# Start of a fused DeltaNet and SwiGLU kernel: weight loads two at a time, idle-time products on TensorE, separate PSUM banks for chunk 0, q loaded behind the first squares

## The chip, the cores and the metric

The kernel runs on one core of a Trainium2 chip. The metric is the device time of one execution, in microseconds (us); the number compared is the median over several executions. One further execution was recorded by the hardware profiler, and all durations below come from it. The engines are PE (TensorE, with PEld for its weight loads), DVE (VectorE), ACT (ScalarE), POOL (GpSimd) and SP (SyncE, which here only issues transfers). Each engine works through its own list of instructions in order.

## The reference

Two blocks follow each other. The first is a delta rule over 768 time steps, for 4 batches times 8 heads of size 48. The second is a feed-forward block on the 3072 rows that come out, 384 wide inside the model and 1536 wide in the hidden layer.

```python
k_n = k / (norm(k, axis=-1) + 1e-06)
state = zeros((B, H, D, D))                      # B=4, H=8, S=768, D=48
for t in range(S):
    y[:, :, t] = einsum('bhd,bhde->bhe', q[:, :, t], state)
    v_old = einsum('bhde,bhd->bhe', state, k_n[:, :, t])
    state = state + beta[:, :, t] * einsum('bhd,bhe->bhde', k_n[:, :, t], v[:, :, t] - v_old)

x = y.transpose(0, 2, 1, 3).reshape(3072, 384)
g = x @ w_gate                                   # 384 x 1536
out = (g * sigmoid(g) * (x @ w_val)) @ w_out     # 1536 x 384
```

q, k, v and beta are 32-bit numbers; the three weight matrices arrive as 64-bit numbers.

## The kernel before

Time is cut into 12 chunks of 64 steps. Inside a chunk the recurrence becomes a triangular system: the Gram matrix of the keys is built, its triangular part is inverted (the result is called Z), and then products give the corrected values `u`, the output `y` and the new state. The feed-forward block of a chunk runs on the same core, in between the attention products of later chunks. From about 85 us on PE is never idle for long; the start, which the change edits, is different, because chunk 0 has to get through a chain of dependent steps before there is any feed-forward work to do.

All instructions are put in an order written out by hand, engine by engine (`tc.manual_schedule`). So the order in which the Python calls stand is the order on every engine, and an instruction that waits holds back all that stand behind it on its engine. The start runs as follows.

1. Loads. `k` of chunks 0 and 1 is issued from the SP and ACT queues before anything else (chunk 0 in four transfers, line 188; chunk 1 by `load_k`, line 135). `beta` goes from POOL (line 395). Then, all on SP: `q` of chunk 0 into `qpad[0]`, `k` of chunks 2 and 3, `q` of chunk 1, `v` of chunk 0 (line 181), the first 12 pieces of weights (`stage`, line 258), `v` of chunk 1, and two more pieces.
2. Norms of the keys (`norms`, lines 368 to 380): DVE squares and sums, POOL takes a power (line 380). Between the two calls stands a memset of the padding columns of `qpad[0]` (line 1580).
3. PE transposes `k` of chunk 0 (line 470), ACT copies the result (line 472), PE forms the Gram products (lines 623 and 624), and the same for chunk 1. ACT and DVE pick out the diagonal blocks (line 629), and DVE transposes them (line 1603).
4. `first_scale` joins the norms with the Gram blocks (lines 422 to 649), and `first_substitution` (lines 665 and 671) runs 15 steps of two DVE operations each; `first_z` and `spread_z` (lines 675 to 686) write Z. Meanwhile PE transposes `q` and the later keys and forms their Gram products (line 486). The last of these is that of `q` of chunk 1.
5. `advance(0)`: PE multiplies Z into the lower blocks (line 695) and into `v` (line 904), then refines the result three times, half by half (`by_par`, line 924, with a DVE addition, line 1288, after every half), and forms `y` of chunk 0 with the products of `by_par` again (also line 924). `y` has two halves called `par`. Half 0 is copied by ACT (line 999); half 1 is copied in four parts by ACT and DVE in turn (line 1002), all from one PSUM bank. Then PE transposes `y` into `x` (line 1017), and ACT copies it in two parts (line 1020). After that the first feed-forward product (`gate_val`, line 1217) can start.

The weights arrive as 64-bit words in staging places and are turned into 32-bit numbers by two ACT operations (`power_step`, lines 270 and 276) and three DVE operations (`convert`, lines 287 to 307) a piece. `converts_first` does this for the first six pieces by hand, among the steps of `advance(0)`.

PSUM is used as two double banks with the tags `px` and `py`, and four single banks `ffn0` to `ffn3`, which `ps_ffn` hands out in turn or by number.

Of the kernel before, what the change touches and what calls it, by code (L numbers as in the profile page):

```python
# [20 lines left out]
def kernel(  # L21
# [47 lines left out]
    def ps_pair(name, tag):  # L69

        return psum.tile([128, 2, 512], FP32, name=name, tag=tag, bufs=1)
# [58 lines left out]
    def halves(x, c, b):  # L130
        return x[NB * b : NB * b + NB, :, c * C : (c + 1) * C, :]
# [43 lines left out]
    def load_v(c):  # L175
        vin[c] = work.tile([128, 2, NB, NJ, D], FP32, name="vin", bufs=2)
        for b in range(2):
            src = halves(v, c, b).rearrange("bp (j par) p d -> par p (bp j) d", par=2)
            for par in range(2):
                s = 64 * (b ^ par)  # L180
                nc.sync.dma_start(
                    out=vin[c][s : s + 64, par].rearrange("p bp j d -> p (bp j) d"),
                    in_=src[par],
                )

    for bp in range(NB):
        for b, engine in enumerate((nc.sync, nc.scalar)):
            engine.dma_start(
                out=knp[0][64 * b : 64 * b + 64, bp, :, 0:D],
                in_=halves(k, 0, b)[bp].rearrange("h p d -> p h d"),  # L190
            )
    load_k(1, (nc.sync, nc.scalar))
    beta_b = const.tile([128, NG, R], FP32, name="beta_b")
    wg_sb = const.tile([128, KT, DFF], FP32, name="wg_sb")
# [48 lines left out]
        at = max(before) if before else LATE.get(name, -1)  # L243
        freed_by.setdefault(at, []).append(n)

    def stage(n, queue=nc.sync):
        _, src, t, f0, m = pieces[n]
        name, lo = place_of[n]
        if name not in places:
            if name == "p_sb":  # L250
                places[name] = words(p_places[0])
            else:
                places[name] = work.tile(
                    [128, 2 * PIECE], U32, name="staged", tag=name, bufs=1
                )
        place = places[name][:, lo : lo + 2 * m]
        staged[n] = place
        queue.dma_start(
            out=place, in_=src[t * 128 : (t + 1) * 128, f0 : f0 + m].bitcast(U32)
        )  # L260
# [88 lines left out]
    def half_of(x):  # L349
        return slice(64 * x, 64 * x + 64)  # L350
# [13 lines left out]
    def norms(c):  # L364

        ksq = work.tile([128, NB, H, D], FP32, name="ksq", tag="r", bufs=2)
        x = knp[c][:, :, :, 0:D]
        nc.vector.tensor_tensor(out=ksq, in0=x, in1=x, op=ALU.mult)
        n = n_t[0][:, c].rearrange("p (par bp j) -> p par bp j", par=2, bp=NB)
        ksq_v = ksq.rearrange("p bp (j par) d -> p par bp j d", par=2)  # L370
        for to, of, par in (
            (slice(0, 128), slice(0, 128), 0),
            (half_of(0), half_of(1), 1),
            (half_of(1), half_of(0), 1),
        ):
            nc.vector.tensor_reduce(
                out=n[to, par], in_=ksq_v[of, par], axis=mybir.AxisListType.X, op=ALU.add
            )
        n = n_t[0][:, c]
        nc.gpsimd.tensor_tensor(out=n, in0=n, in1=half[:, 0:HH], op=ALU.pow)  # L380
# [225 lines left out]
    def unread():  # L606

        p = ps_pair("p_t", "px")[:, 0]
        for n in range(88):
            q_ = QUADS[n % 4][0]  # L610
            nc.tensor.matmul(p[q_, 0:1], half[q_], half[q_, 0:1])

    def first_gram(c, tag):

# [239 lines left out]
    def advance(c):  # L854
# [7 lines left out]
        if c > 0:  # L862
# [23 lines left out]
        p_u = recur(ps_pair("p_u", "px"))  # L886

        def new_u(name):
            return work.tile([128, 2, NB, NJ, D], FP32, name=name, tag="r", bufs=2)

        def single(bank):
            return [
                p[:, 0 : NB * NJ * D].rearrange("p (bp j d) -> p bp j d", bp=NB, j=NJ)
                for p in banks("p_u", bank)
            ]

        v0 = new_u("uu" if c > 1 else "v0")
        if c == 0:
            p_n = banks("p_n", "py")
# [2 lines left out]
                n_copy(c, p_n, par)  # L902
        for bp, j, par, b, first in every():
            nc.tensor.matmul(  # L904
                p_u[half_of(b), par, bp, j],
                zt[half_of(b ^ par), par, bp, j],
                r[half_of(b ^ par), par, bp, j],
                start=first,
                stop=True,
                skip_group_check=True,  # L910
            )
# [7 lines left out]
        def by_par(p, stationary, moving, flip, start):  # L919
            for par in range(2):  # L920
                for bp in range(NB):
                    for j in range(NJ):
                        for b in range(2):
                            nc.tensor.matmul(  # L924
                                p[par][half_of(b ^ par * flip), bp, j],
                                stationary[half_of(b), par, bp, j],
                                moving[half_of(b), par, bp, j],
                                start=start and bp + j == 0,
                                stop=True,
                                skip_group_check=True,  # L930
                            )
                yield par

        if c < 2:
            yield MORE
            uu = new_u("uu")
            p_n = single(2) if c == 0 else [p_u[:, par] for par in range(2)]
# [53 lines left out]

        if 0 < c < NCH - 1:
            of_state()
        each = range(NB) if c == 0 else (slice(0, NB),)
        y = work.tile([128, NB, NJ, 2, D], FP32, name="y", tag="r", bufs=2)
        if c == 0:
            for par in by_par(p_y, pq, uu, 1, True):
                if par == 0:
                    nc.scalar.copy(y[:, :, :, 0], p_y[0])
            for bp in range(NB):  # L1000
                for b, copy in ((0, nc.scalar.copy), (1, nc.vector.tensor_copy)):
                    copy(y[half_of(b), bp, :, 1], p_y[1][half_of(1 - b), bp])
        else:
            p_of_u()
            nc.scalar.copy(y[:, :, :, 0], p_y[:, 0])
            for b in range(2):
                nc.scalar.copy(y[half_of(b), :, :, 1], p_y[half_of(1 - b), 1])
# [4 lines left out]
        p_f = ps_pair("p_f", "py")[:, :, 0 : KT * 128]  # L1012
        p_f = p_f.rearrange("p bp (t n) -> p t bp n", t=KT)
        for bp in range(NB):
            for t in range(KT):
                at = slice(t * 128, (t + 1) * 128)
                nc.tensor.transpose(p_f[:, t, bp], y_f[:, bp, at], ident)  # L1017
        x_v = xts[c].rearrange("p t (bp n) -> p t bp n", bp=NB)
        for bp in each:
            nc.scalar.copy(x_v[:, :, bp], p_f[:, :, bp])  # L1020
        if 2 <= c < NCH - 1 and (c + 1) // 2 in n_t:
            scale_v(c + 1)
        yield
# [543 lines left out]
    with tc.manual_schedule(  # L1567
# [9 lines left out]
        load_beta()  # L1577
        first_tiles()
        norms(0)
        nc.vector.memset(qpad[0][:, :, :, D:DP], 0.0)  # L1580
        norms(1)
        load_q(0)
        load_k(2)
        load_k(3)
        load_q(1)
        load_v(0)
        for n in range(12):
            stage(n)
        load_v(1)
        stage(12)  # L1590
        stage(13)
        copy_a, copy_v = nc.scalar.copy, nc.vector.tensor_copy
        unread()
        turned(0, False, 0)
# [7 lines left out]
        spread_beta(copy_a)  # L1602
        nc.vector.transpose(first_of["mb"][:, 0 : R * R], first_of["flat"])
        first_scale(first_n())
        low_copies(0, p_g[0])
        turned(0, True, 0)
        low_copies(1, p_g[1])
# [19 lines left out]
        scale_v(0)  # L1627
        for steps_of in first_q:
            next(steps_of)
        new_nt(0, qpad[1].rearrange("p bp h d -> p (bp h d)"))  # L1630
        zb_1 = work.tile([128, R, R], FP32, name="zb", bufs=1)
        new_nt(1, zb_1.rearrange("p k i -> p (k i)"))
# [94 lines left out]
```

## Time and profile before

| what | value |
|---|---|
| median of 3 executions | 705.18 us (705.01 to 708.58) |
| profiled execution, its own time | 704.64 us |
| its span, first to last instruction | 702.4 us |
| mean granted TensorE clock | 0.993 |
| PE busy | 681.3 us (97% of the span) |
| DVE busy | 472.4 us (67%) |
| ACT busy | 258.8 us (37%) |
| POOL busy | 51.0 us (7%) |
| DMA | 62.32 MB, mean 89 GB/s |

PE is busy in 97% of the span, so what time it loses is found in stretches. The stretches in which PE works less lie in the first 60 us. A start time in the views below is counted from the first instruction; where a row says "issue", the engine stood without waiting for anything that the profile shows.

### The profile page before, as it was taken

What the parts mean: (1) busy time and instruction counts of PE and PEld (TensorE: products, weight loads), DVE (VectorE), ACT (ScalarE), POOL (GpSimd) and SP (SyncE); (2) the same over time, 40 slices, a digit from 0 to 9 for tenths busy, and PEclk for the clock granted to TensorE, in tenths of its full rate; (3) what the DMA queues carried; (4) which work ended last, traced back from release to release, by engine and by line L of the source; (5) the groups of instructions that cost most, each with busy time, mean ns of one, the idle gap of its engine ahead of it and who ended that gap; (6) DMA issues with size and microseconds to landing.
All of it is one profiled execution on the core that took longest, in us unless ns stands there. A gap on an engine that the chain in (4) does not pass through costs nothing.

```text
span 702.4 us, 25672 instructions
## 1 busy us (share of the span) xinstructions
PE 681.3 (97%) x11432; PEld 641.7 (91%) x11432; DVE 472.4 (67%) x1096; ACT 258.8 (37%) x542; POOL 51.0 (7%) x39
## 2 busy tenths in 40 slices
PE   7599999999999999999999999999999999999997
PEld 6588788756999999999999999999999999999997
DVE  5866779798899848987469787379844345333341
ACT  4456666203533433235233235232153132142230
POOL 6000031105000030000300001200000000000000
PEclk9899999999999999999999999999999999999999
DMA  8873715006461522465333274143241131221210
GB/s 140 246 197 85 217 50 185 1 22 149 136 128 24 108 67 59 77 128 93 71 90 70 58 136 81 35 114 83 55 107 48 44 85 57 54 62 46 68 46 23
DMA packets 143886, 62.32 MB, mean 89 GB/s; under 512 B 123008, under 2 KB 126080, under 8 KB 143776
## 3 DMA queue, kind: packets, MB, share of 16 engines
q1 hardware_dynamic: 141552, 60.19, 36.7%
q8 instruction: 90, 1.47, 0.9%
q10 hardware_dynamic: 2096, 0.39, 0.3%
q0 software_dynamic: 128, 0.10, 0.1%
q14 instruction: 20, 0.16, 0.1%
HBM read 53.58 MB, written 7.08 MB: 86 GB/s over the span
## 4 chain that ended last, share of the span: by engine, by line
PE 91%; DVE 3%; ACT 3%; issue 1%; POOL 1%; DMA 1%; SPq 0%; DVEq 0%; ACTq 0%; POOLq 0%
PE ffn L1121 43%; PE ffn L1327 20%; PE ffn L1217 8%; PE ffn L1244 4%; PE p_g L486 3%; PE p_u L904 2%; PE p_s L972 2%; PE p_r L866 2%; PE p_y L960 1%; PE p_y L875 1%; PE ffn L924 1%; PE p_f L1017 1%; POOL n_t L380 1%; PE p_u L924 1%; DMA kn<-in_k_dram 1%
## 5 line engine op out<-in xcount | busy, mean ns | idle before, releaser
L1121 PE MATMUL ffn<-x_ffn,wg_sb 128*128 128x128 f32 x840 | 128.3, 275 | 0.3 <-ACT x_ffn L1020 0.2
L1121 PE MATMUL ffn<-x_ffn,wv_sb 128*128 128x128 f32 x840 | 128.1, 275 | 0.0
L1121 PEld LDWEIGHTS ffn<-x_ffn,wg_sb 128*128 128x128 f32 x840 | 111.1, 192 | 0.6 <-ACT ffn L1177 0.3
L1121 PEld LDWEIGHTS ffn<-x_ffn,wv_sb 128*128 128x128 f32 x840 | 110.7, 192 | 0.0
L1151 ACT ACTIVATE sil<-ffn 128x256 f32<-128x256 f32 x120 | 46.1, 384 | 132.6 <-PE ffn L1121 127.8
L1327 PE MATMUL ffn<-wo_sb,h_f 128*128 128x192 f32 x480 | 83.4, 327 | 0.0
L1156 DVE TENSOR_TENSOR h_f<-sil,ffn 128x256 f32<-128x256 f32 x120 | 49.6, 418 | 48.8 <-ACT sil L1151 46.3
L1327 PEld LDWEIGHTS ffn<-wo_sb,h_f 128*128 128x128 f32 x480 | 78.1, 190 | 0.4
L1288 DVE TENSOR_TENSOR ffn<-ffn,p_sb 128x512 f32<-128x512 f32 x58 | 40.4, 696 | 44.6 <-ACT ffn L1177 43.6
L1121 PE MATMUL ffn<-x_t,h_f 128*128 128x128 f32 x480 | 61.0, 280 | 0.2 <-ACT ffn L1134 0.2
L1121 PEld LDWEIGHTS ffn<-x_t,h_f 128*128 128x128 f32 x480 | 56.2, 191 | 1.4 <-ACT ffn L1134 0.3
L564 DVE TENSOR_TENSOR zb<-zb,tmp 128x31 f32<-128x31 f32 (+15 forms) x155 | 53.1, 343 | 5.3
L558 DVE TENSOR_TENSOR tmp<-zb,mb 128x31 f32<-128x31 f32 (+15 forms) x155 | 52.7, 340 | 4.0
L774 POOL TENSOR_TENSOR n_b<-mb,half 128x32 f32<-128x32 f32 x5 | 30.0, 6002 | 338.5 <-DVE mb L528 338.5
L1288 DVE TENSOR_TENSOR o_sb<-o_sb,ffn 128x192 f32<-128x192 f32 x49 | 17.2, 351 | 51.2 <-PE ffn L1327 49.1
L1134 ACT COPY ffn<-ffn 128x512 f32<-128x512 f32 x30 | 17.1, 571 | 63.8 <-PE ffn L1121 57.4
L1327 PE MATMUL ffn<-last_k,h_f 128*128 128x192 f32 x200 | 35.9, 327 | 0.0
L1217 PE MATMUL ffn<-x_ffn,wg_sb 128*128 128x256 f32 x144 | 34.0, 383 | 0.0
L1217 PE MATMUL ffn<-x_ffn,wv_sb 128*128 128x256 f32 x144 | 33.8, 382 | 0.0
L1327 PEld LDWEIGHTS ffn<-last_k,h_f 128*128 128x128 f32 x200 | 32.9, 190 | 0.1
L1121 PE MATMUL ffn<-x_ffn,p_sb 128*128 128x128 f32 x216 | 30.1, 282 | 1.2 <-issue 1.2
L1217 PEld LDWEIGHTS ffn<-x_ffn,wv_sb 128*128 128x128 f32 x144 | 27.0, 190 | 3.7
(272 smaller groups left out, 1063.6 us busy)
## 6 DMA issues: line engine op xcount, KB each, us to landing
h_f<-w_s SPq DMA_DIRECT2D x60, 256.0 KB, 2.8
p_sb<-w_s SPq DMA_DIRECT2D x27, 256.0 KB, 2.7
vin<-in_v_dram SPq DMA_DIRECT2D x48, 96.0 KB, 3.4
out_dram<-o_sb SPq DMA_DIRECT2D x48, 96.0 KB, 2.2
kn<-in_k_dram SPq DMA_DIRECT2D x19, 192.0 KB, 4.4
zt<-in_moe_w_out_dram SPq DMA_DIRECT2D x6, 384.0 KB, 3.3
qpad<-in_q_dram SPq DMA_DIRECT2D x36, 64.0 KB, 3.0
w_s<-h_f SPq DMA_DIRECT2D x7, 256.0 KB, 3.5
```

Of the source, the lines that this page charges most:

```text
L486: nc.tensor.matmul(p_v[par][half_of(b if of_q else b ^ par), bp, j], kt[c][half_of(par), bp, j, b], xt[half_of(par), bp, j, b],)
L558: nc.vector.tensor_tensor(out=t_v, in0=zb[:, 0 : j + 1, j : j + 1].to_broadcast([128, j + 1, m]), in1=mb[:, j : j + 1, j + 1 : R].to_broad ...
L564: nc.vector.tensor_tensor(out=zb[:, 0 : j + 1, j + 1 : R], in0=zb[:, 0 : j + 1, j + 1 : R], in1=t_v, op=ALU.add,)
L774: nc.gpsimd.tensor_tensor(out=n, in0=mb.rearrange("p j i -> p (j i)")[:, 0 : R * R : R + 1], in1=half, op=ALU.pow,)
L1121: nc.tensor.matmul(p[:, u], w(u), moving, start=start and u == 0, stop=True, skip_group_check=True,)
L1134: nc.scalar.copy(p_y, p_x)
L1151: nc.scalar.activation(sil[:, n].rearrange("p (i n) -> p i n", i=2), p[:, 0:2], ACTF.Silu)
L1156: nc.vector.tensor_tensor(out=h_of(c, f, j), in0=sil[:, n].rearrange("p (i n) -> p i n", i=2), in1=p[:, 2:4], op=ALU.mult,)
L1217: nc.tensor.matmul(ps[name][:, i], w_sb[:, t, (f + i) * 128 : (f + i + 1) * 128], xts[c][:, t], start=(t == 0 and i == 0), stop=(t == KT - 1),
L1244: nc.tensor.matmul(p_o, hs[c, f - f % 2][:, f % 2, bp * 128 : (bp + 1) * 128], wo_sb[:, f], start=(f == 0), stop=(f == FT - 1),)
L1288: nc.vector.tensor_tensor(out=out, in0=a, in1=b, op=ALU.add)
L1327: nc.tensor.matmul(p[x, part], a(f - f % 2)[:, f % 2], b(f), start=not begun and f == 0, stop=f == FH - 1, skip_group_check=True,)
```

## The change

It has five parts.

- `k` of chunk 0 is loaded by two transfers of 192 KB in place of four of 96 KB.
- The memset of `qpad[0]` moves from between the two `norms` calls to between the squares and the sums of `norms(0)`, and it is one column wider. That column is also written by the load of `q` of chunk 0, so this load, on SP, now waits for the memset, and SP's later transfers stand behind it.
- `stage` gets an argument `after`. With it POOL copies one column from the staging place of piece `after` to that of piece `n`, before the transfer of `n`: the copy waits until piece `after` has landed, and the transfer waits for the copy. Pieces 2 to 13 get it, with `n - 2`. These calls stand behind `first_scale` now, so POOL's copies come behind its work for the norms.
- `warm(3)` puts three products of 128x128 by 128x512, whose result nobody reads, on PE between the Gram products of `q` and `advance(0)`. They go into the double bank `px`.
- In chunk 0 the part of `y` with `par` 1 and `bp` 1 goes into a third single bank (`ffn2`). ACT copies the two parts of `bp` 0 and DVE the two of `bp` 1. `x` is transposed into `ffn0` and `ffn3` in place of the double bank `py`; ACT copies one and DVE the other.

```diff
-    for bp in range(NB):
-        for b, engine in enumerate((nc.sync, nc.scalar)):
-            engine.dma_start(
-                out=knp[0][64 * b : 64 * b + 64, bp, :, 0:D],
-                in_=halves(k, 0, b)[bp].rearrange("h p d -> p h d"),
-            )
+    load_k(0, (nc.sync, nc.scalar))
...
-    def stage(n, queue=nc.sync):
+    def stage(n, after=None, queue=nc.sync):
...
+        if after is not None:
+            nc.gpsimd.tensor_copy(place[:, 0:1], staged[after][:, 0:1])
...
         n = n_t[0][:, c].rearrange("p (par bp j) -> p par bp j", par=2, bp=NB)
+        if c == 0:
+            nc.vector.memset(qpad[0][:, :, :, D - 1 : DP], 0.0)
...
+    def warm(count):
+
+        p = ps_pair("p_t", "px")[:, 0]
+        for _ in range(count):
+            nc.tensor.matmul(p, ident, kts[0][:, 0:512])
...
-            for par in by_par(p_y, pq, uu, 1, True):
+            third = single(2)[0]
+            for par in range(2):
+                for bp in range(NB):
+                    p = third if par and bp else p_y[par]
+                    for j in range(NJ):
+                        for b in range(2):
+                            nc.tensor.matmul(
+                                p[half_of(b ^ par), bp, j],
+                                pq[half_of(b), par, bp, j],
+                                uu[half_of(b), par, bp, j],
+                                start=j == 0 and (bp == 0 or par == 1),
+                                stop=True,
+                                skip_group_check=True,
+                            )
                 if par == 0:
                     nc.scalar.copy(y[:, :, :, 0], p_y[0])
-            for bp in range(NB):
-                for b, copy in ((0, nc.scalar.copy), (1, nc.vector.tensor_copy)):
-                    copy(y[half_of(b), bp, :, 1], p_y[1][half_of(1 - b), bp])
+            for b in range(2):
+                nc.scalar.copy(y[half_of(b), 0, :, 1], p_y[1][half_of(1 - b), 0])
+                nc.vector.tensor_copy(y[half_of(b), 1, :, 1], third[half_of(1 - b), 1])
...
+        if c == 0:
+            p_f = [ps_ffn([128, KT, 128], "p_f", 3 * bp) for bp in range(NB)]
+        else:
+            p_f = ps_pair("p_f", "py")[:, :, 0 : KT * 128]
+            p_f = p_f.rearrange("p bp (t n) -> p t bp n", t=KT)
...
+        if c == 0:
+            nc.scalar.copy(x_v[:, :, 0], p_f[0])
+            nc.vector.tensor_copy(x_v[:, :, 1], p_f[1])
+        else:
+            nc.scalar.copy(x_v, p_f)
...
         norms(0)
-        nc.vector.memset(qpad[0][:, :, :, D:DP], 0.0)
         norms(1)
...
-        for n in range(12):
-            stage(n)
-        load_v(1)
-        stage(12)
-        stage(13)
...
         first_scale(first_n())
+        for n in range(12):
+            stage(n, n - 2 if n > 1 else None)
+        load_v(1)
+        stage(12, 10)
+        stage(13, 11)
...
         for steps_of in first_q:
             next(steps_of)
+        warm(3)
```

More of the change, by code (lines that the diff above doesn't have):

```diff
@@ L885, in advance @@
             yield
-        p_u = recur(ps_pair("p_u", "px"))
         def new_u(name):
@@ L895, in single @@
             ]
+        p_u = recur(ps_pair("p_u", "px"))
+        p_u_of = [p_u[:, 0], p_u[:, 1]]
         v0 = new_u("uu" if c > 1 else "v0")
@@ L904, in advance @@
             nc.tensor.matmul(
-                p_u[half_of(b), par, bp, j],
+                p_u_of[par][half_of(b), bp, j],
                 zt[half_of(b ^ par), par, bp, j],
@@ L936, in advance @@
             uu = new_u("uu")
-            p_n = single(2) if c == 0 else [p_u[:, par] for par in range(2)]
+            p_n = single(2) if c == 0 else p_u_of
             for n in range(3):
@@ L993, in advance @@
             of_state()
-        each = range(NB) if c == 0 else (slice(0, NB),)
         y = work.tile([128, NB, NJ, 2, D], FP32, name="y", tag="r", bufs=2)
         if c == 0:
-            for par in by_par(p_y, pq, uu, 1, True):
+            third = single(2)[0]
[12 more added lines that the diff above has]
+                            )
                 if par == 0:
                     nc.scalar.copy(y[:, :, :, 0], p_y[0])
-            for bp in range(NB):
-                for b, copy in ((0, nc.scalar.copy), (1, nc.vector.tensor_copy)):
-                    copy(y[half_of(b), bp, :, 1], p_y[1][half_of(1 - b), bp])
+            for b in range(2):
+                nc.scalar.copy(y[half_of(b), 0, :, 1], p_y[1][half_of(1 - b), 0])
+                nc.vector.tensor_copy(y[half_of(b), 1, :, 1], third[half_of(1 - b), 1])
         else:
@@ L1011, in advance @@
         xts[c] = ffn_pool.tile([128, KT, TOK], FP32, name="x_ffn")
-        p_f = ps_pair("p_f", "py")[:, :, 0 : KT * 128]
-        p_f = p_f.rearrange("p bp (t n) -> p t bp n", t=KT)
+        if c == 0:
[3 more added lines that the diff above has]
+            p_f = p_f.rearrange("p bp (t n) -> p t bp n", t=KT)
         for bp in range(NB):
@@ L1016, in advance @@
                 at = slice(t * 128, (t + 1) * 128)
-                nc.tensor.transpose(p_f[:, t, bp], y_f[:, bp, at], ident)
+                p = p_f[bp][:, t] if c == 0 else p_f[:, t, bp]
+                nc.tensor.transpose(p, y_f[:, bp, at], ident)
         x_v = xts[c].rearrange("p t (bp n) -> p t bp n", bp=NB)
-        for bp in each:
-            nc.scalar.copy(x_v[:, :, bp], p_f[:, :, bp])
+        if c == 0:
[3 more added lines that the diff above has]
+            nc.scalar.copy(x_v, p_f)
         if 2 <= c < NCH - 1 and (c + 1) // 2 in n_t:
```

## The prediction

> **What bounds the kernel now.** First the page: PE is busy 97% of the span, and only the first slices of row PE are below 9. I therefore read only the start. Next the chain that ended last, from 0 to 110 us (start, length, what):
>
> ```profile
> 1.64 6.00 DMA kn<-in_k_dram
> ...
> 10.58 6.73 POOL n_t L380 x2
> ...
> 28.36 1.25 DVE mb L675
> 29.64 0.78 ACT zt L684
> ...
> 33.64 1.53 issue
> 35.17 0.61 PE p_u L904 x25
> ...
> 36.34 8.44 PE ffn L924 x231
> 44.77 0.69 issue
> ```
>
> The keys land at 7.64, the norms end on POOL at 17.30, the substitution gives Z at 29.64, then PE's products follow. PE alone, in order of time, shows what it waited for (in brackets):
>
> ```profile
> 27.00 0.92 PE L486 MATMUL ffn<-qt,kt 64*64 64x64 f32 x24 [2.58 <-issue]
> ...
> 35.17 0.57 PE L904 MATMUL p_u<-vin,zt 64*64 64x48 f32 x25 [1.53 <-issue]
> 36.34 3.28 PE L924 MATMUL ffn<-v,qpad 64*64 64x48 f32 x64 [0.60 <-ACT v L913]
> 39.41 4.28 PE L924 MATMUL ffn<-uu,qpad 64*64 64x48 f32 x128
> ```
>
> "Issue" is a wait for nothing that the profile shows. The stalls stand 128 matmul records (256 instructions) apart or a multiple, and the instruction queue q8 moves one packet in the us around 24, 32 and 43, just before they end. I read them as instruction fetches queued behind weights. The third view is the work by stretches of one us; the last three columns are granted clock, DMA share, GB/s:
>
> ```profile
> 24.00:25.00 1.00, 0.42 (x31) 0.32 (x21) 0.89 (x4) 1.00 (x3) 0.00 (x0) 1.00 0.76 219
> 26.00:27.00 1.00, 0.00 (x0) 0.00 (x0) 0.90 (x4) 0.00 (x0) 0.00 (x0) 0.79 1.03 352
> 28.00:29.00 1.00, 0.00 (x0) 0.00 (x0) 0.93 (x3) 0.00 (x0) 0.00 (x0) 0.50 1.01 379
> 38.00:39.00 1.00, 1.00 (x26) 1.00 (x22) 0.51 (x1) 1.00 (x2) 0.00 (x0) 0.50 1.09 241
> ```
>
> PE runs at half clock from 26.6 to 33.4 and from 36.8 to 40.2 (the ends worked out from means such as 0.79), while DMA is full. So the start loses to late keys, to fetches, and to the clock.
>
> **Part 1: keys of chunk 0, q behind the squares.** The first squares start at 7.75, when the later SP half of k lands (issued 1.64, 6.0 us). Two transfers instead of four end k's issue at about 1.5 instead of 2.5, and q, on SP from 3.29, no longer shares the engines. Ahead of the squares there are then only k of two chunks and beta, 0.88 MB, which at the 165 to 195 GB/s of 3 to 7 us are through by about 7. Chunk 0 has the head start: I estimate 6.0 (5.2 to 7.0). From there two paths lead to the join at line 422 (before, 17.33). Norms: 9.6 us as before plus the memset, 0.3 (row 1580, 0.27), so 9.9. Gram: it had 0.42 us to spare, 9.2; but now all eight transposes follow the landing where four were done before, and four took 1.08: 10.25. This one ends last: 16.25, a gain of 1.1. On SP, q, k of 2 and 3, q of 1 and v of 0 follow the memset, from about 7.3. The 2.9 MB from the first k to that v took from 2 to 22 us, some 145 GB/s, and that pace, not SP, spaced them; so v's end and the first weight (19.8) stay; PE's last Gram product may come a us later, which the wait for Z hides. POOL's 12 copies run beside the substitution. The nearest row is the 128x32 copy on POOL, 0.24 us; if each of the six before Z stopped DVE for so long it would be 1.4, if none, 0. I take 0.3. **Z: 0.8 earlier** (2.0 earlier to 0.5 later).
>
> **Part 2: weights two at a time, and fetches.** The first weights, with few in flight, landed in 3.9 and 3.7 us; with eight, in 6.5:
>
> ```profile
> h_f<-in_moe_w_gate_dram SPq DMA_DIRECT2D x1, 256.0 KB, 3.9
> h_f<-in_moe_w_gate_dram SPq DMA_DIRECT2D x1, 256.0 KB, 6.5
> ```
>
> With two in flight I take 3.2 (quiet 256 KB loads later: 2.8) plus 0.4 for POOL's copy and the SP issue: 3.6 a pair. Pieces 0 and 1 start at 19.8, so 2 and 3 land at 27, 4 and 5 at 30.6, 10 and 11 at 41.4, v of 1 at about 45, 12 and 13 at 46. ACT takes pieces 0 and 2 at 33, pieces 6 on at about 48 and 12 at about 52 (before: 52.9 and 56.87): covered, by 6 us for piece 12. [...] A packet keeps one engine for about 1.3 us (8.3% of 16 engines for one us), then about 1 us passes; only the queueing before it, 1 to 2 us, is what fewer weights save. While PE runs at full clock it also has less time before the next block. So of the 1.53 I leave 1.1, of the 0.69 I leave 0.1.
>
> **Part 3: the unread products.** Full-rate rows of 128x256 give 1.49 us for three (6 records, line 1217), so three of 128x512 take 3.0. PE's Gram work ends near 25.7 with a fetch stall cut to about 1 us, so they fill 25.7 to 28.7, just ahead of the first product with Z (29.7). [...] The row decides: from 23.2 to 26.6 PE worked only 1 us and the clock fell; from 33.4 to 36.8 it worked 1.3 of 3.4 (38%), and it fell again. With the products that first stretch is 70% busy. At full clock 64 products with Z take 1.16 (row 486) instead of 2.2, and p_u 1.15. From Z to the end of p_u: 0.84 + 1.16 + 1.1 stall + 1.1 = 4.2 instead of 6.14: **1.9 earlier** (0.8 to 3.0). The refinements (36.34 to 44.29, 7.95) at the 0.93 a half of the later rows take 6 x 0.93 + 1.2 = 6.75: **1.2 earlier** (0 if the clock falls once more: the stall and the copy of v leave PE about half busy there, between 38% and what surely holds).
>
> **Part 4: y and x.** Last refinement to first feed-forward product: 44.29 to 49.50, 5.2. The four y copies took turns (46.46 to 47.89); now ACT and DVE take two each, 0.7. But DVE's two stand behind the conversion of pieces 0 and 2 (1.75), and its x copy behind that of piece 4 (1.2). Along DVE: 1.75 + 0.7 + 1.2 + 0.55, then PE: 4.25. **0.95 earlier**, of which 0.6 is the fetch (0.3 to 1.6).
>
> **Part 5: what comes later.** Pieces 12 to 22, v of 1 and 2, and q of 2, some 3.9 MB, move from before 48 to about 42 to 54. There PE is dense, and its next blocks end near 45.3 and 48.7. [...] **0.7 later** (0 to 2). After that PE is bound by its work (10.0 busy in each 10 us from 90), and the shift stays to the end.
>
> Sum: -0.8 - 1.9 - 1.2 - 0.95 + 0.7 = -4.15. The profiled 704.64 (span 702.4) becomes 700.5; it stood 0.54 below the median 705.18, which becomes **701.0**.
>
> **Rivals.**
> A (the sum above, 699 to 702.5): 0.62.
> B, the clock still falls, or fetches take as long: the 1.2 and half of the 1.9 are lost: -4.15 + 2.15 = -2.0, 703.2. For it: p_u's stall and the copy of v. Against it: the stretch before Z is filled. 0.15.
> C, the moved burst costs what the throttle saved: two stalls of 1.5 between 45 and 55: 704.0. For it: DMA was empty there before. [...] 0.13.
> D, slower: the throttle makes weights late. ACT needs piece 12; it lands at 19.8 + 7P, P the time of a pair. At P = 5.3 that is 56.9, where it was needed before, and nothing is gained; from 5.8 the run is over 3.5 slower, at 6 it is 5 slower, 710. For it: 6.5 us with eight in flight. Against it: 3.9 with few. 0.10.
>
> **Numbers.** 0.5%, 3.5 us, is about what a measurement can tell (the runs spread by that). A gives 0.50 faster and 0.12 same; B 0.02 and 0.13; C 0.13 same; D 0.10 slower. Faster 0.52, same 0.38, slower 0.10. The range 697.5 to 705.6 takes in the ends of A, then B and C, and leaves out D and A's best ends.
>
> **What would show it.** Squares at about 6; Z near 28.8; granted clock 1.0 from 23 to 45; no 2.58 wait in line 486; first product of line 1217 near 44.7; a new "issue" wait near 49. Wrong, if the products start after 28, if ACT waits for a DMA at pieces 8 to 13, or if the first product of line 1217 comes earlier and the end does not.

## The result: 0.4% faster, and the profile after

| | runs | median us | lowest to highest | profiled execution (span) |
|---|---|---|---|---|
| before | 20 | 706.63 | 705.01 to 709.44 | 704.64 (702.4) |
| changed | 20 | 703.46 | 701.89 to 707.33 | 707.33 (705.6) |

The ratio of changed to before is 0.9958, with a 95% interval of 0.9944 to 0.9971: 2.0 to 4.0 us faster, about 3.0. The forecast was 4.15 faster. The change is real, but at 0.42% it stays below the 0.5% that the prediction asked of "faster", to which it gave 0.52, and counts as its "same", to which it gave 0.38.

The profiled execution of the changed kernel happens to be the longest of its 20, so its waits are read here and its total is not. One of the kernels below, u_yx, has the same program on PE up to the end of the refinements and gives a second look at that stretch.

PE of the changed kernel in order of time (start, length, what; in brackets the idle time before it and what ended it), at the places that the prediction had named:

```profile
5.85 1.94 PE L469 MATMUL ffn<-ident,kn 128*128 128x128 f32 x8 [2.00 <-DMA kn<-in_k_dram]
...
13.60 0.21 PE L629 MATMUL p_g<-kt 64*32 64x64 f32 x1 [1.46 <-issue]
...
27.02 0.57 PE L485 MATMUL ffn<-qt,kt 64*64 64x64 f32 x23 [2.02 <-issue]
27.52 2.84 PE L616 MATMUL p_t<-kt,ident 128*128 128x512 f32 x6
30.39 1.35 PE L700 MATMUL p_n<-zt,a_sb 64*64 64x64 f32 x61
...
34.50 0.68 PE L910 MATMUL p_u<-vin,zt 64*64 64x48 f32 x31 [2.25 <-issue]
35.77 3.65 PE L930 MATMUL ffn<-v,qpad 64*64 64x48 f32 x64 [0.59 <-ACT v L919]
...
49.52 1.53 PE L1242 MATMUL ffn<-x_ffn,wg_sb 128*128 128x256 f32 x6 [0.18 <-DVE x_ffn L1043]
...
56.68 1.01 PE L880 MATMUL p_y<-state,qt 64*64 64x48 f32 x51 [1.76 <-issue]
```

The keys are there at 5.8, as forecast. Everything after that differs from the forecast. The fetch stall ahead of line 485 (486 before) is 2.02 where about 1 was expected, so the unread products (line 616) run from 27.52 to 30.36, up to the very moment when ACT has written its part of Z (30.34). The stall in p_u is 2.25 and not 1.1. The first gate product starts at 49.52, where it stood before (49.50).

The same execution by stretches of one us (busy PE, PEld, DVE, ACT, POOL; granted clock; DMA share; GB/s):

```profile
26.00:27.00 1.00, 0.00 (x0) 0.00 (x0) 0.89 (x4) 0.00 (x0) 0.00 (x0) 1.00 0.45 129
28.00:29.00 1.00, 1.00 (x4) 0.47 (x3) 0.93 (x2) 0.00 (x0) 0.18 (x1) 1.00 0.33 53
33.00:34.00 1.00, 0.00 (x0) 0.00 (x0) 0.85 (x2) 0.00 (x0) 0.00 (x0) 1.00 0.49 180
38.00:39.00 1.00, 1.00 (x24) 1.00 (x22) 0.32 (x1) 1.00 (x2) 0.15 (x1) 0.50 0.35 131
55.00:56.00 1.00, 0.00 (x0) 0.00 (x0) 1.00 (x5) 1.00 (x4) 0.00 (x0) 1.00 0.97 336
```

DMA is no longer full while PE waits for code (0.45 at 26, where it was 1.03), and still PE waits. The clock is whole at 28, where it was half. But PE then idles through the whole of the us from 33, and the clock is half from 35.6 to 42.4: the half clock has moved from before Z to the refinements behind it. In the us from 55, PE idles once more for nothing that the profile shows, while DMA is full; before, no such stall stood here. These "issue" stalls are called waits for code from here on, because a packet of the instruction queue q8 starts 2.3 to 2.9 us before each of them ends. In the trace of the changed kernel 125 to 128 matmul records lie between one of them and the next, or a multiple of that; a block is one such stretch of PE's program, and its end is called a boundary.

### The profile page after: what moved, and what is told of

The parts are those of the page before. It is cut to its first block, busy times and chain, and to the rows that moved or that the text cites. A ratio compares the mean times of both kernels' runs of the same rounds, so it can differ in the third digit from the quotient of the medians.

```text
span 705.6 us, 25724 instructions
## 1 busy us (share of the span) xinstructions
PE 684.5 (97%) x11438; PEld 642.9 (91%) x11438; DVE 473.0 (67%) x1097; ACT 258.7 (37%) x541; POOL 54.0 (8%) x51
## 3 DMA queue, kind: packets, MB, share of 16 engines
q8 instruction: 90, 1.47, 0.9%
## 4 chain that ended last, share of the span: by engine, by line
PE 94%; issue 2%; DVE 2%; ACT 1%; DMA 1%; DVEq 0%; ACTq 0%
PE ffn L1146 42%; PE ffn L1352 20%; PE ffn L1242 9%; PE ffn L1269 4%; PE p_g L485 3%; PE p_u L910 2%; PE p_s L978 2%; PE p_r L871 2%; PE p_y L880 2%; PE ffn L930 1%; PE p_y L966 1%; PE p_u L930 1%; PE p_f L1039 1%; PE ffn L469 1%; PE p_j L848 1%
## 5 line engine op out<-in xcount | busy, mean ns | idle before, releaser
L1146 PEld LDWEIGHTS ffn<-x_ffn,wg_sb 128*128 128x128 f32 x840 | 111.1, 192 | 0.7 <-ACT ffn L1202 0.4
L1146 PEld LDWEIGHTS ffn<-x_ffn,wv_sb 128*128 128x128 f32 x840 | 110.7, 192 | 0.0
L1242 PEld LDWEIGHTS ffn<-x_ffn,wg_sb 128*128 128x128 f32 x144 | 26.6, 190 | 4.3 <-DVE wg_sb L304 0.4
```

The lines of the kernel that those rows point to most:

```text
L1146: nc.tensor.matmul(p[:, u], w(u), moving, start=start and u == 0, stop=True, skip_group_check=True,)
L1242: nc.tensor.matmul(ps[name][:, i], w_sb[:, t, (f + i) * 128 : (f + i + 1) * 128], xts[c][:, t], start=(t == 0 and i == 0), stop=(t == KT - 1),
```

## The experiments

All ratios are to the kernel before on the same chip. A difference between two kernels is the difference of their ratios, with the two intervals combined as independent, turned into us at 706 us a run. "Gate" is the start of the first product of line 1242 in the profiled execution (49.52 in the changed kernel).

### Undoing one part of the changed kernel

**u_warm** leaves out the three unread products.

```diff
         for steps_of in first_q:
             next(steps_of)
-        warm(3)
```

> The changed kernel without the three unread products; all else as changed. The changed kernel stands 3.0 us below the one before (ratio 0.9958). Theory 'the products hold the clock': the granted clock falls to 0.5 before the first product with Z, and the gain shrinks by about 2 us, to -1.0. Rival 'the clock is lost anyway, later, in the stall of p_u and the copy of v' (the changed kernel's own profile had 0.5 from 35.8 to 42.2): without the products the loss only moves, and the gain stays within 0.7 us of -3.0.

Measured: median 701.92 in 11 runs, ratio 0.9946 [0.9925, 0.9967]. Without the products the kernel is 0.8 us faster than with them, plus or minus 1.8: no gain from them can be seen, and the 2 us of the theory are ruled out. The rival comes nearer: the loss only moves. Its PE, in order of time:

```profile
26.39 0.57 PE L485 MATMUL ffn<-qt,kt 64*64 64x64 f32 x23 [0.65 <-issue]
...
30.13 2.12 PE L700 MATMUL p_n<-zt,a_sb 64*64 64x64 f32 x61 [3.16 <-ACT zt L689]
32.13 1.94 PE L910 MATMUL p_u<-vin,zt 64*64 64x48 f32 x62
34.68 2.07 PE L930 MATMUL ffn<-v,qpad 64*64 64x48 f32 x64 [0.61 <-ACT v L919]
```

The mechanism shows. PE idles 3.16 us until Z, the clock falls (half from 30.2 to 33.6), p_n takes 2.12 instead of 1.35, and p_u 1.94. But p_u now has no stall at all (62 products in 1.94 without a wait): while PE crawls, the next code arrives. PE begins the refinements at 34.68, earlier than the 35.77 of the changed kernel, with the clock whole (64 products in 2.07 instead of 3.65), and the gate is at 45.43. With the faster products in front of it, PE waited 2.25 us for that code; without them, not at all.

**u_thr** takes the throttle away: the first 14 loads are issued at once, in their old place, and POOL's copies are gone.

```diff
         load_v(0)
+        for n in range(12):
+            stage(n)
+        load_v(1)
+        stage(12)
+        stage(13)
...
         first_scale(first_n())
-        for n in range(12):
-            stage(n, n - 2 if n > 1 else None)
-        load_v(1)
-        stage(12, 10)
-        stage(13, 11)
         low_copies(0, p_g[0])
```

> The changed kernel with the first 14 pieces of weights loaded without the waits, where the kernel before has them. Theory 'two in flight shortens the fetches before Z and in p_u': the wait of line 485 is back at 2.5 us and that of p_u at 1.5 or more; but the new wait near 55 us (1.8 us in the changed kernel's profile) goes away, so the net loss is small: -2.5 of the -3.0 stays. Rival 'the throttle is where the gain is': -0.5 or less stays, because the unread products then start after 27.5 us and run into the first product with Z.

Measured: 706.47 in 12 runs, 1.0003 [0.9987, 1.002]. The throttle is worth 3.2 us (plus or minus 1.5), about as much as the whole change. That 2.5 us of the gain would stay, as the first theory had it, is wrong, and the rival is right about the time. PE:

```profile
27.52 0.57 PE L485 MATMUL ffn<-qt,kt 64*64 64x64 f32 x23 [2.56 <-issue]
28.02 2.84 PE L616 MATMUL p_t<-kt,ident 128*128 128x512 f32 x6
30.80 1.16 PE L700 MATMUL p_n<-zt,a_sb 64*64 64x64 f32 x64
...
35.03 0.68 PE L910 MATMUL p_u<-vin,zt 64*64 64x48 f32 x31 [2.58 <-issue]
```

With eight loads in flight, the stalls are 0.5 and 0.3 us longer (2.56 for 2.02, 2.58 for 2.25), the first product with Z has to wait for the unread ones until 30.80 although ACT's part of Z is ready at 30.13, and p_u resumes at 35.03. The gate is at 50.01. The throttle's price is visible too: u_thr has no stall near 56, so the stall there in the changed kernel belongs to the moved burst. Up to the gate the trace accounts for some 0.5 us, against 3.2 in the times; set against u_yx, the second look at the changed kernel's start, the refinements end 2.5 us later in u_thr (45.66 for 43.19). How the 3.2 divide is not shown, since single executions differ by as much.

**u_q** puts back the four transfers of k of chunk 0 and the early q.

```diff
-    load_k(0, (nc.sync, nc.scalar))
+    for bp in range(NB):
+        for b, engine in enumerate((nc.sync, nc.scalar)):
+            engine.dma_start(
...
-        if c == 0:
-            nc.vector.memset(qpad[0][:, :, :, D - 1 : DP], 0.0)
...
         norms(0)
+        nc.vector.memset(qpad[0][:, :, :, D:DP], 0.0)
         norms(1)
```

> The changed kernel with k of chunk 0 in four transfers and q straight behind k, as before. Theory 'the earlier keys are eaten by a fetch in the Gram products of chunk 1' (in the changed kernel's profile the squares start 1.9 us earlier, but a wait of 1.5 us in line 628 leaves the join at 17.2 against 17.3): nothing is lost, -3.0 stays within 0.5. Rival, the prediction's step: Z comes 0.8 to 1.1 us later, -2.0 stays.

Measured: 705.31 in 12 runs, 0.999 [0.9971, 1.0009]: this part is worth 2.3 us (plus or minus 1.6), where the theory had nothing and the rival about 1. Its trace shows the squares at 7.78, two us later than in the changed kernel, but Z at 29.68, against 29.54 there and 29.27 to 29.33 in u_warm, u_thr and u_yx, whose start is the same: later by 0.1 to 0.4. Of the two us of earlier keys, little reaches Z, and yet undoing them costs time. What carries the 2.3 us was not located.

**u_yx** puts back the old banks and copies of y and x.

```diff
-            third = single(2)[0]
...
-            for b in range(2):
-                nc.scalar.copy(y[half_of(b), 0, :, 1], p_y[1][half_of(1 - b), 0])
-                nc.vector.tensor_copy(y[half_of(b), 1, :, 1], third[half_of(1 - b), 1])
+            for bp in range(NB):
+                for b, copy in ((0, nc.scalar.copy), (1, nc.vector.tensor_copy)):
+                    copy(y[half_of(b), bp, :, 1], p_y[1][half_of(1 - b), bp])
...
-        if c == 0:
-            nc.scalar.copy(x_v[:, :, 0], p_f[0])
-            nc.vector.tensor_copy(x_v[:, :, 1], p_f[1])
```

> The changed kernel with the y and x copies of chunk 0 as before (one bank for y's second half, a double bank for x). Theory, the prediction's step: from the end of the last refinement to the first product of line 1217/1242 takes 5.0 us instead of 4.25 and the end comes 0.6 to 0.95 later: -2.2 stays. Rival 'ACT's conversions, which run without a break from the copy of the state, set the pace after 52 us and hide it': -3.0 stays.

Measured: 704.67 in 12 runs, 0.9981 [0.996, 1.0001]; 1.6 us lost, plus or minus 1.7, so not separated from nothing. The trace is sharper: from the end of the last refinement (43.19) to the gate (47.65) it takes 4.46, where the theory had 5.0, and in the changed kernel 4.35 (45.17 to 49.52). The banks themselves are worth about 0.1 us.

As the second look at the changed kernel's start, u_yx shows the same picture a little milder: a stall of 1.64 in line 485, of 1.99 in p_u, and half clock from 36.5 to 39.9, so that the refinements take 7.96 us (35.23 to 43.19).

```profile
33.96 0.68 PE L910 MATMUL p_u<-vin,zt 64*64 64x48 f32 x31 [1.99 <-issue]
35.23 2.64 PE L930 MATMUL ffn<-v,qpad 64*64 64x48 f32 x64 [0.59 <-ACT v L919]
```

The four differences add up to 6.3 us, more than the 3.0 of the whole: the parts overlap, and the changed kernel's own error stands in all four.

### Shifting where PE's code blocks end

If PE's wait for code falls where it does because of the count of instructions ahead of it, a few instructions more or fewer should move it. The 88 tiny products at the very start (32x32 by 1, before the keys land) are the place: one fewer is two matmul records, four instructions of PE (b85 below, the kernel before with three fewer, has 11,426 matmul records and as many weight loads, for 11,432).

```diff
-        for n in range(88):
+        for n in range(94):
             q_ = QUADS[n % 4][0]
```

**w94** is the changed kernel with 94; **n94** is the same without warm(3); **b94** is the kernel before with 94; **w82** is the changed kernel with 82.

> The changed kernel with 94 instead of 88 tiny products at the very start (1.0 to 4.0 us, before any key has landed): every later boundary of 256 instructions on PE comes 12 matmul records earlier in the program. So 35 instead of 29 records of a block are done when PE stands at the first product with Z. Theory 'the fetch in p_u is asked for about 32 records into a block, and so only once Z is there': now it is asked for before Z, the wait of 2.0 to 2.6 us in p_u goes away, PE no longer idles, the clock stays at 1.0 through the refinements, and the end comes 2 to 4 us earlier than the changed kernel's: ratio 0.990 to 0.993. Rival 'DMA is simply slow there, whenever the fetch is asked for': the wait moves by 12 records but stays about 2 us, ratio 0.995 to 0.997.

> As w94, without the three unread products. [...] Theory 'the products are worth the half clock once the fetch no longer stands behind them': n94 is 1 to 2 us slower than w94. [...]

> The kernel before with 94 instead of 88 tiny products at the start, nothing else. 36 instead of 24 records of the block lie ahead of the first product with Z. Theory of the early request: the wait of 1.5 us in p_u goes away although all weights are in flight, the clock does not fall a second time, ratio about 0.996 (1.5 for the wait and 1.2 for the clock). Rival 'the weights in flight make the fetch slow': the wait stays at 1 us or more, ratio 0.999 to 1.001.

> The changed kernel with 82 tiny products: boundaries 12 records later, 17 records of the block ahead of Z. Control for w94: theory of the request 32 records in: the wait in p_u, now 46 records into p_u, is 1.6 to 2.2 us still, as the request comes 0.2 us later and the boundary 0.4 us later. If a shift as such helped, it would be gone here too.

| | median us (runs) | ratio | stall in 485 | stall in p_u | gate |
|---|---|---|---|---|---|
| w94 | 703.57 (12) | 0.9965 [0.9942, 0.9988] | 1.87 | 0.49 | 46.42 |
| n94 | 707.07 (12) | 1.0001 [0.9983, 1.0019] | 1.49 | 0.79 | 49.34 |
| b94 | 709.12 (12) | 1.0023 [1.0, 1.0046] | 3.51 | 1.16 | 49.91 |
| w82 | 699.54 (2) | 0.9895 [0.9848, 0.9943] | 1.56 | 1.82 | 47.53 |

PE of w94:

```profile
17.83 1.86 PE L469 MATMUL ffn<-ident,qpad 128*128 128x128 f32 x8 [2.34 <-ACT a_sb L639]
...
28.74 0.80 PE L485 MATMUL ffn<-qt,kt 64*64 64x64 f32 x35 [1.87 <-issue]
29.47 2.84 PE L616 MATMUL p_t<-kt,ident 128*128 128x512 f32 x6
32.24 1.16 PE L700 MATMUL p_n<-zt,a_sb 64*64 64x64 f32 x64
...
34.22 0.90 PE L910 MATMUL p_u<-vin,zt 64*64 64x48 f32 x43 [0.49 <-issue]
35.69 2.07 PE L930 MATMUL ffn<-v,qpad 64*64 64x48 f32 x64 [0.57 <-ACT v L919]
```

The stall in p_u is down to 0.49, and the clock stays whole through the refinements (64 products in 2.07). But it was not the early request that did this. The packet that ends the stall starts at 31.75, no earlier than in the changed kernel (31.65); PE only reaches the end of its block later, at 33.7 instead of 32.25. The time did not follow either; 0.990 to 0.993 had been expected. The shift put a boundary ahead of the transposes of q: they start at 17.83 instead of 16.05, and the 2.34 before them is put down to ACT, but a packet starts at 14.85, and n94 shows a wait at the same place as "issue" (1.46). The clock then fell to half from 17.9 to 21.3. So the unread products start at 29.47 only, and the first product with Z comes at 32.24, 2 us after Z. One good boundary was paid for with a bad one.

n94 shows it from the other side: it is u_warm with six tiny products more, and it is 3.9 us slower (plus or minus 2.0). It is also 2.5 us slower than w94 (plus or minus 2.1), as the theory for n94 had it: here the unread products do seem to help, though the boundaries behind Z differ between the two as well. In b94 the stall in p_u stays, at 1.16, against the theory, and it is 1.6 us slower than the kernel before, at the edge of its interval. w82 shows the 1.6 to 2.2 that were expected of its stall (1.82). So six tiny products more or fewer, which do no work for the result, are worth about as much as the change.

w82 has two runs only. **w82b** is the same kernel with more runs, **b85** the kernel before with 85, and **w85** and **n85** are the changed kernel with 85, with and without the unread products. Three tiny products are six matmul records, and so are the three unread ones. So n85 (three tiny ones fewer and no unread ones) puts the boundaries behind Z where w82b (six tiny ones fewer) has them, and w85 puts them where u_warm has them.

```diff
-        for n in range(88):
+        for n in range(82):
             q_ = QUADS[n % 4][0]
```

> The kernel of w82 (the changed kernel, 82 tiny products at the start) once more, timed in full. Theory 'the place of PE's boundaries of 256 instructions decides': w82's trace shows 0.2 us of 'issue' waits on PE after 62 us, where the changed kernel shows 3.2 and the kernel before 2.1, so it stays 2 to 3 us ahead of the changed kernel: ratio 0.990 to 0.993. Rival 'two runs by chance': ratio 0.9958 as the changed kernel.

> The changed kernel without the three unread products and with 85 tiny products: boundaries after Z as in w82b. Theory 'the products only cost their shift': the same time as w82b within 1 us, ratio 0.990 to 0.993. Theory 'the products hold the clock': 1 to 2 us slower than w82b.

> The changed kernel, all five parts, with 85 tiny products: the three products' 12 instructions are taken out again ahead of them, so that all later boundaries stand where they stand in the kernel before and in u_warm. Theory 'the products cost their shift': the 'issue' waits after 62 us are 2.1 instead of 3.2, and it is 1 us faster than the changed kernel, ratio 0.9945, equal to u_warm. Theory 'the products hold the clock and are worth it': faster than u_warm by 1 or more, ratio 0.993 or less.

> The kernel before with 85 tiny products instead of 88, nothing else: after the place of the three unread products its boundaries stand where they stand in w82. Theory of the boundaries: the 'issue' waits after 62 us fall from 2.1 to about 0.2, ratio 0.997. Rival: the boundaries are worth something only with the other parts: ratio 0.999 to 1.001.

| | median us (runs) | ratio | stall in p_u | waits for code on PE after 62 us | gate |
|---|---|---|---|---|---|
| w82b | 700.02 (6) | 0.9921 [0.9897, 0.9944] | 1.33 | 1.0 | 45.88 |
| n85 | 700.40 (6) | 0.9925 [0.9899, 0.995] | 0.89 | 0.5 | 47.76 |
| w85 | 702.02 (8) | 0.9949 [0.9927, 0.9972] | 2.18 | 1.4 | 47.50 |
| b85 | 704.39 (12) | 0.9984 [0.9964, 1.0004] | 1.66 | 1.7 | 51.87 |
| changed (88) | 703.46 (20) | 0.9958 [0.9944, 0.9971] | 2.25 | 3.2 | 49.52 |

With the alignment behind Z held, no effect of the products can be seen: n85 is 0.3 us slower than w82b (plus or minus 2.4), and u_warm 0.2 faster than w85 (plus or minus 2.2). w82b beats both kernels, as expected: 5.6 us (4.0 to 7.3) under the kernel before, and 2.6 (plus or minus 1.9) under the changed one. Its PE, to be laid beside that of the changed kernel:

```profile
27.71 0.45 PE L485 MATMUL ffn<-qt,kt 64*64 64x64 f32 x11 [1.37 <-issue]
28.08 2.84 PE L616 MATMUL p_t<-kt,ident 128*128 128x512 f32 x6
30.86 1.16 PE L700 MATMUL p_n<-zt,a_sb 64*64 64x64 f32 x64
...
34.02 0.55 PE L910 MATMUL p_u<-vin,zt 64*64 64x48 f32 x19 [1.33 <-issue]
35.13 2.07 PE L930 MATMUL ffn<-v,qpad 64*64 64x48 f32 x64 [0.57 <-ACT v L919]
```

And of n85, without the products:

```profile
30.18 2.12 PE L700 MATMUL p_n<-zt,a_sb 64*64 64x64 f32 x61 [3.49 <-ACT zt L689]
...
34.35 0.55 PE L910 MATMUL p_u<-vin,zt 64*64 64x48 f32 x18 [0.89 <-issue]
35.46 2.79 PE L930 MATMUL ffn<-v,qpad 64*64 64x48 f32 x64 [0.57 <-ACT v L919]
```

With the products, p_n is 1 us faster, yet p_u resumes at 34.02 against 34.35: of the 1 us, 0.3 is left. This holds for all kernels with a stall there: with two loads in flight p_u goes on between 34.0 and 34.6 in all nine of them, and with all loads in flight between 34.8 and 35.3 in all four, whatever stands ahead of the boundary. The shift seems to work in the tail too. The waits of PE after 62 us (line waited for: us in all, times, longest), in the changed kernel and then in w82b:

```profile
PE p_j L848 <- issue: 2.2, 2, 1.7
PE p_u L910 <- issue: 0.6, 1, 0.6
PE p_j L757 <- issue: 0.4, 1, 0.4
```

```profile
PE ffn L1146 <- issue: 1.0, 2, 0.9
```

3.2 us of waits for code become 1.0. In the kernel before the same sum was 2.1. b85 missed: it was expected to lose its late waits (0.2 left) and kept 1.7; its ratio cannot be told from 1. w85 came out at 0.9949, near the 0.9945 expected, but its 0.6 us (plus or minus 1.9) under the changed kernel cannot be told from nothing.

One thing stays open. In all three series (before, changed, changed without the unread products) the kernel with fewer tiny products has the lower median. If the place of the boundaries alone decided, a shift by a whole block (64 tiny products) would change nothing, and no such kernel was run; nor was the kernel before with 82.

## Why the prediction was right or wrong

The direction and the order of size were right, but the sum of 4.15 came from terms that did not hold, so that its nearness to the 3.0 measured is in part luck. Step by step:

**Part 1, the keys.** The landing was right (6.0 forecast, 5.8 measured), as was the memset. The step that failed is the Gram path with 16.25 at its end. DVE shows the join and then Z:

```profile
17.23 0.14 DVE L421 TENSOR_SCALAR n_t<-n_t 128x32 f32<-128x32 f32 x1
...
29.54 1.05 DVE L691 TENSOR_SCALAR zt<-mb,m_rows 128x512 f32<-128x512 f32 x2
```

The rest of Z is written by ACT:

```profile
29.54 0.80 ACT L689 ACTIVATE zt<-mb,m_rows 128x256 f32<-128x256 f32 x1 [3.94 <-DVE mb L680]
```

The join is 0.1 us earlier than before (17.33), and Z 0.1 (29.64), not 0.8; in u_warm, u_thr and u_yx Z is 0.3 to 0.4 earlier. What is late next is in the first listing: PE waits 1.46 us for code ahead of line 629 at 13.60, in the Gram of chunk 1. The packet for that block starts at 10.7, no earlier than before (10.35), although the keys come 2 us earlier: before, PE was still at work when the code came. I had not looked for the next block on this stretch. The 0.3 for POOL's copies beside the substitution was too much: one of DVE's operations took 0.32 instead of 0.29, and the others kept their length. Undoing the part costs 2.3 us all the same, through a path that I did not find.

**Part 2, the throttle.** The pair time was right: POOL's first and eleventh copy start at 23.91 and 42.11, five pairs apart, so 3.64 us a pair against the 3.6 forecast. So rival D is out, whose point was 5.3: ACT takes piece 12 at 56.82 without a wait for a DMA.

```profile
56.82 0.44 ACT L267 ACTIVATE wg_sb<-wo_sb 128x256 f32<-128x256 f32 x1
```

The mis-sized term is what fewer weights leave of a fetch: "of the 1.53 I leave 1.1", and 2.25 was measured. From the start of the instruction queue's packet to PE going on, it takes 2.85 and 2.72 us before (24.15 to 27.00 and 32.45 to 35.17), 2.77 and 2.85 in the changed kernel (24.25 to 27.02 and 31.65 to 34.50), and 2.2 to 3.1 at the stalls of line 485 and p_u in all kernels here. Here is the second packet (count, MB, share of the 16 DMA engines), in the stretch of 0.05 us in which it starts: before (32.45:32.50), in the changed kernel (31.65:31.70) and in w94 (31.75:31.80).

```profile
q8 instruction: 1, 0.02, 166.9%
```

```profile
q8 instruction: 1, 0.02, 170.6%
```

```profile
q8 instruction: 1, 0.02, 116.0%
```

I had read that as about 2.3 (1.3 and 1) and given the throttle everything ahead of the packet, 1 to 2 us by my estimate, which no run shows; the throttle does start the second packet 0.8 us earlier (31.65), but PE, at full clock, reaches the end of its block 1.4 us earlier (32.25 instead of 33.64), and the difference is waiting. What sets the start of the packet stays open. It lies 1.8 to 2.9 us after the first write of Z in every kernel, even in w94, where 41 records of the block stand ahead of Z and PE reaches the first product with Z 2 us late. So a request 32 records into a block, which the expectations assumed, does not fit. A request later in the block would fit, and so would one that is held back while PE's instructions wait for Z; no run separates them.

That the waits at the boundaries cost time, as the prediction had it, the shifts bear out: w82b (2.6 us faster than the changed kernel) and n94 (3.9 slower than u_warm) differ from their partners by six tiny products at the start alone, which move the boundaries. What I did not do is take the spacing of 128 matmul records to the end, and lay out every boundary of the changed program before costing anything.

**Part 3, the unread products.** "Wrong, if the products start after 28" was nearly met at 27.52, yet their place was no loss in itself: they end at 30.36, as ACT's part of Z is done, and the first product with Z starts at 30.39 (30.48 before). The mis-sized terms come behind it. "4.2 from Z to the end of p_u" measured 5.64 (29.54 to 35.18), of which the stall alone is 1.15 too much, and the refinements took 9.4 (35.77 to 45.17) in this execution and 7.96 in u_yx, instead of 6.75, because the clock fell once more. It did stay whole before Z, and w82b shows what the refinements take when it stays whole afterwards: 6.4. But n85 and u_warm lose the clock before Z and end as early as w82b and w85. The term of 1.9 plus 1.2 lies outside the intervals of both comparisons, and 0 lies inside: what the faster products save in front of the boundary, the fetch takes back. Only with 94 tiny products is the kernel with the products ahead (w94 by 2.5 us of n94), and there the boundaries behind Z differ too. One reading of the rows was off without consequence: the stretch from 23.2 to 26.6 held 1.2 us of work, not 1.

The clock itself followed the idling, but not the length of one gap. In one profiled execution of each kernel with the products, the clock fell in the refinements or just ahead of them after a p_u stall of 1.82 (w82), 1.98 (u_q), 1.99 (u_yx), 2.18 (w85), 2.25 (changed) and 2.58 (u_thr), and held after 0.49 (w94) and 1.33 (w82b); about 0.6 of waiting for ACT's copy of v follows in each. In n85, without the products, it fell at 36.5 after a stall of only 0.89. I had left rival B only 0.15 for that. Of the rivals B fits the trace best, though it too counts half of the 1.9 as gained. That its 703.2 is so near the median of 703.46 is luck: the kernel before stood 1.45 us higher here than the 705.18 that the prediction started from, and the gain of 3.0 lies halfway between B's 2.0 and A's 4.15.

**Part 4, y and x.** 4.25 forecast from the last refinement to the gate, 4.35 measured. Right in size, and the 0.6 rightly given to the fetch (there is no stall on this stretch now). The banks themselves bring 0.1 by u_yx's trace, not 0.35.

**Part 5, the burst.** Right in kind: a new wait for code where none stood, at 56.68 instead of near 49; absent in u_thr. No run shows the 0.7 of the sum; the trace shows a stall of 1.76 in its place, which ends 2.30 us after a packet starts (54.38). In u_warm, u_q and u_yx the wait in line 880 (883) is 1.11, 0.35 and 0.63. Rival C had two such waits.

**What the sum missed altogether** is that the gain of the start does not stay to the end. "After that PE is bound by its work" and "the shift stays to the end" were the step; PE waits for code behind the gate too, in every kernel: after 62 us 2.1 us in the one before, 3.2 in the changed one, and 0.2 and 1.0 in two executions of the same kernel, w82 and w82b. These two show what that does. w82b reaches the gate 1.65 us earlier (45.88 for 47.53) and yet has the longer span (699.6 for 699.2): 1.4 us of the difference are waits for code behind the gate (2.9 for 1.5). In all fourteen profiled executions, the span less the start of the gate and less the waits for code behind it is 650.2 to 651.7 us. So these two sums, the start and the late waits, hold nearly all of the differences between the traces. In the changed kernel's long execution the late waits are 5.0, against 2.1 before. In the four traces where this was followed to the end (before, changed, w82b, u_q), a packet of the instruction queue starts 2.4 to 2.9 us before each wait after 62 us ends. One of these waits falls between 250 and 256 us in every one of the fourteen traces, with 0.2 to 1.7 us: shifting the boundaries changes its size and not where it is. What is slow there is not shown.

The 12 instructions that the change adds to PE's program (six matmul records with their weight loads) shift every later boundary, which the prediction did not count either. Taking them out again (w85) brings 0.6 us, plus or minus 1.9. The count is not all of it, since u_q and u_yx, with the changed kernel's count, show 1.9 and 3.3 us of waits after 62 us.

## What to carry to other kernels

In the dense, tiny matmuls of this start PE waited for code, in the changed kernel 2.25 us in p_u alone: lay out where each block of 128 matmul records ends, and do not count an edit that makes PE faster ahead of such an end as a gain until the fetch is earlier too. Before and after any small edit, try the kernel with a few harmless instructions more and fewer at its start; here that moved the time about as much as the edit did (2.6 us one way, 3.9 the other). Do not carry a gain at the start to the end of the program before the waits behind it are counted. Judge an edit that also changes the instruction count only against a version with the count restored, as w85 and n85 do for the products.

## What the runs showed of the hardware

- From the start of the packet on the instruction queue to PE going on, 2.2 to 3.1 us passed at the stalls of line 485 and p_u, with two 256 KB loads in flight or with eight. The page of the changed kernel counts 11,438 matmul records, as many weight loads and 90 packets of that queue (1.47 MB), so 127 matmul records a packet. 64 of 64x48 took 1.08 us at full clock (line 904 in the kernel before, from 57.18 to the next product at 58.26), so 128 of them last an estimated 2.2 us, no longer than the fetch.
- Six tiny products more or fewer at 1 to 4 us moved the time of a 705 us program by up to 3.9 us (plus or minus 2.0; n94 and u_warm).
- The granted clock fell to 0.50 after gaps of PE of 1.82 and 0.57 us (w82) and held after 1.33 and 0.57 (w82b); but in n85 it fell after 0.89 and 0.57. The length of a single gap did not decide.
- A kernel whose granted clock was lower on the mean over its runs (n85, 0.9927) was as fast, within 2.4 us, as one that kept it (w82b, 0.996).
- With two 256 KB loads in flight a pair took 3.64 us, about 144 GB/s; single loads with eight in flight had taken 6.5.
